# Streamed weight units brought in as two half-partition transfers, and the first four input tiles handled in the plain order

## The chip, the cores and the metric

The kernel runs on one core of a Trainium2 chip. The metric is the device time of one execution in microseconds (us). Before the change three executions took 1972.40, 1976.64 and 1977.27 us; their median is 1976.64.

## What is computed

The reference adds three things: the input x (2048 rows of 1024), a recurrent attention layer over the normalized input, and a dense two-layer network over the same normalized input. Cut to what matters:

```python
xn = layernorm(x)                                  # no scale, no shift
# attention with memory: 64 segments of 32 rows, one after the other
for s in range(64):
    h = concatenate([mem, xn[32*s:32*s+32]])       # 8 memory rows and 32 new rows
    q, k, v = h @ Wq, h @ Wk, h @ Wv               # 1024 -> 32 heads of 128
    p = softmax(masked(q @ k.T * 128**-0.5))
    o = (p @ v) @ Wo                               # 4096 -> 1024
    mem = o[:8]                                    # the next segment needs this
    A[s] = o[8:]
B = gelu(xn @ w1 + b1) @ w2 + b2                   # 1024 -> 3584 -> 1024
out = x + A + B
```

Because a segment's memory rows come out of the segment before, the 64 segments run in order, and each of them passes through all of Wq, Wk, Wv and Wo. In bfloat16 these four are 32 MB, which is more than the on-chip memory holds beside the rest.

## The kernel before

**The dense part** comes first, up to about 420 us. It normalizes x in 16 tiles of 128 rows, transposes each on PE (`turn_x`, L358), and computes the dense network in four groups of four tiles: L481 is the first matrix product, L530 and L563 the second. The results, and the transposed input, are kept in DRAM for the recurrent part.

Before the first product of the first group the first four tiles must be normalized and turned (L436 to L453). Each tile needs statistics on VectorE (`ln_stats`, L323), a square root on ScalarE (`ln_sqrt`, L329), a reciprocal on VectorE (`ln_rstd`, L335), and an application of mean and factor. For tiles 0 to 2 the application is on ScalarE (`ln_apply_scalar`, L346), for tile 3 on VectorE (`ln_apply`, L338). Tiles go one after the other: while one is applied and turned, the statistics of the next are made. PE turns a tile in eight transposes (L362), and two copies (L365), one on VectorE and one on ScalarE, take the result out of PSUM. The scratch tiles for the normalized rows and for the turned rows in PSUM exist twice.

Transfers of this part are nearly all begun by SP, in the order of the program. For the first half of w1, `load_w1` (L292) begins 16 of them: eight for the left half of its columns, then the bias b1 (L302), then eight for the right half. Then come three copies of the masks (L177), four small loads of the memory rows (L308), the bias b2 (L313), the second half of w1, and w2 (L317).

**The recurrent part** is the loop over 64 segments (L658). The four weight matrices are cut into 64 units of 128 partitions by 2048 columns (512 KB, a partition's row 4096 bytes). `pass_order` (L53) lists the units in the order in which each segment uses them. 46 of them stay on the chip for the whole run. The other 18, marked `S` in `PLACED` (L68) and spread over the order, are streamed again for every segment from a contiguous copy of each in DRAM (`copies`, L192, called Wc in the profile). One of the 18 (`IN_PSUM`, L73) is kept in PSUM and is put back by two copies on VectorE (L226) in place of a transfer. Of another (`HALF`, L74) one half stays on the chip, so that its transfer has 256 KB.

Streamed units go through a ring of six tiles (`STREAM_BUFS`, L50). `start_stream` (L220) takes the next tile of the ring and has SP begin the transfer into it (L229):

```python
c0 = 1024 if streams[started] == HALF else 0
nc.sync.dma_start(out=t[:, c0:2048], in_=copies[streams[started]])
```

It is called six times before the loop (L549), and then by `unit_done` (L640) whenever a streamed unit's last product has been issued; so six units are ahead of PE, being transferred or waiting to be used. SP holds a transfer back until PE has finished with the tile, and until the earlier transfer into that tile has landed. Every transfer that SP begins also uses one of eight semaphores, in turn.

PE multiplies a unit with the segment's rows in four products that fill the four quarters of PSUM's partitions (L682 for Wq, Wk, Wv; L861 for Wo). Each contracts over all 128 partitions of the unit. Between them stand the small products of attention (L785 to L841), and the copies that take the results out of PSUM (L725, L848, L940). L940 copies the segment's new memory rows and comes once at the end of every segment but the last.

GpSimd (POOL) begins the recurrent part's small transfers: loads of the next segment's rows (L237, L242), loads of the dense result (L911, L936), and stores. Only at the end do SP and ScalarE store pieces too (L979).

Of the kernel before, what the change touches and what calls it, by code (L numbers as in the profile page):

```python
# [10 lines left out]
BF16 = mybir.dt.bfloat16  # L11
# [67 lines left out]
def kernel(  # L79
# [59 lines left out]
    def slab(place):  # L139
        if place in low:  # L140
            return low[place]
        return slabs.tile([P, 2048], BF16, name="u", tag=place)
# [77 lines left out]
    def start_stream():  # L220
        nonlocal started
        if started < len(streams):
            t = slab(RING[started % STREAM_BUFS])
            if streams[started] == IN_PSUM and "kept" in nxt:
                for b in range(2):
                    nc.vector.tensor_copy(out=t[:, 1024 * b:1024 * b + 1024], in_=nxt["kept"][:, b, :])  # L226
            else:
                c0 = 1024 if streams[started] == HALF else 0
                nc.sync.dma_start(out=t[:, c0:2048], in_=copies[streams[started]])  # L229
            stream_tiles.append(t)  # L230
            started += 1

# [38 lines left out]
    with tc.tile_pool(name="ma", bufs=2) as ma, tc.tile_pool(name="mps", bufs=6, space=PSUM) as mps:  # L271
# [19 lines left out]

        def load_w1(half):  # L292
            for kt in range(KT):
                w1_sb.append(slab(f"w1_{8 * half + kt}")[:, 0:F // 2])
            for c in (0, 1) if half == 0 else (None,):
                for kt in range(KT):
                    cs = slice(0, F // 2) if c is None else slice(F // 4 * c, F // 4 * c + F // 4)
                    nc.sync.dma_start(
                        out=w1_sb[8 * half + kt][:, cs], in_=w1_v[:, kt, F // 2 * half:F // 2 * (half + 1)][:, cs]
                    )  # L300
                if c == 0:
                    nc.sync.dma_start(out=b1rows[:, :], in_=B_b1.rearrange("(fc p) -> fc p", p=P))  # L302

        b1rows = ma.tile([FC, P], BF16, name="b1rows", bufs=1)
        load_w1(0)
        masks_out()
        for j in range(4):
            nc.sync.dma_start(  # L308
                out=o_sb[32 * j + NX:32 * j + 32, 0:8, :],
                in_=mem0[:, 256 * j:256 * j + 256].rearrange("m (h e) -> m h e", h=8),  # L310
            )
        b2row = ma.tile([1, DM], BF16, name="b2row", bufs=1)
        nc.sync.dma_start(out=b2row[:, :], in_=B_b2.rearrange("(o d) -> o d", o=1))  # L313
        load_w1(1)
# [11 lines left out]
                nc.vector.bn_stats(out=stats[:, c, :], in_=xt[:, c * 512:c * 512 + 512])  # L326
            nc.vector.bn_aggr(out=mv[:, tt, :], in_=stats[:, :, :])

        def ln_sqrt(t0, t1):  # L329
            nc.scalar.activation(  # L330
                out=rstd[:, t0:t1], in_=mv[:, t0:t1, 1:2].rearrange("p t o -> p (t o)"), func=ACT.Sqrt,
                bias=eps_t[:, :], scale=1.0,
            )

        def ln_rstd(t0, t1):  # L335
            nc.vector.reciprocal(out=rstd[:, t0:t1], in_=rstd[:, t0:t1])

        def ln_apply(tt):  # L338
            xn = ma.tile([P, DM], BF16, name="ln_xn")
            nc.vector.tensor_scalar(  # L340
                out=xn[:, :], in0=xtoks[tt], scalar1=mv[:, tt, 0:1], scalar2=rstd[:, tt:tt + 1],
                op0=ALU.subtract, op1=ALU.mult,
            )
            return xn

        def ln_apply_scalar(tt):  # L346

            xn = ma.tile([P, DM], BF16, name="ln_xn")
            shift = mv[:, tt, 0:1]
            nc.vector.tensor_scalar(  # L350
                out=shift, in0=shift, scalar1=rstd[:, tt:tt + 1], scalar2=-1.0, op0=ALU.mult, op1=ALU.mult,
            )
            nc.scalar.activation(
                out=xn[:, :], in_=xtoks[tt], func=ACT.Identity, bias=shift, scale=rstd[:, tt:tt + 1],
            )
            return xn

# [76 lines left out]
            ]  # L434

        xnT = new_xnT(0)  # L436
        def begin(tt):
            ln_stats(tt, xtoks[tt])
            ln_sqrt(tt, tt + 1)

        def normed(tt):
            ln_rstd(tt, tt + 1)
            return ln_apply_scalar(tt) if tt < 3 else ln_apply(tt)

        begin(0)
        xns = []
        for tt in range(4):
            if tt < 3:
                begin(tt + 1)
            xns.append(normed(tt))  # L450
            if tt > 0:
                turn_x(tt - 1, xns[tt - 1], xnT)
        turn_x(3, xns[3], xnT)  # L453
        keep_xT(0, xnT)

        b1col = ma.tile([P, FC], F32, name="b1col", bufs=1)
# [6 lines left out]
        for tg in range(4):  # L463
# [46 lines left out]
            if not last:  # L510
                xnT = new_xnT(tg + 1)
                for t in range(4):
                    xtoks[4 * tg + 4 + t] = load_x(4 * tg + 4 + t)
                if tg == 0:
                    for unit, c in copies.items():
                        fetch(c, unit)
                    fetch_resident(*low)
                for t in range(4):
                    ln_stats(4 * tg + 4 + t, xtoks[4 * tg + 4 + t])
                ln_sqrt(4 * tg + 4, 4 * tg + 8)  # L520
                ln_rstd(4 * tg + 4, 4 * tg + 8)
                for t in range(4):
                    ttg = 4 * tg + t
                    xn = ln_apply(ttg + 4)
                    rsb = xtoks[ttg]
                    for nb in range(2):
                        cs = slice(nb * 512, (nb + 1) * 512)
                        ps = mps.tile([P, 512], F32, name="ps")
                        for fc in range(FC):
                            nc.tensor.matmul(  # L530
                                ps[:, :],
                                lhsT=gts[fc // 4][:, fc % 4, t * P:(t + 1) * P],
                                rhs=w2_sb[fc // 2][:, fc % 2, cs],
                                start=(fc == 0),
                                stop=(fc == FC - 1),
                            )
                        nc.vector.tensor_tensor(out=ps[:, :], in0=ps[:, :], in1=b2bc[:, cs], op=ALU.add)
                        nc.vector.tensor_tensor(out=rsb[:, cs], in0=ps[:, :], in1=rsb[:, cs], op=ALU.add)
                        if nb == 1:
                            turn_x(ttg + 4, xn, xnT)  # L540
                    keep_R(ttg, rsb)
                keep_xT(tg + 1, xnT)
                for t in range(4):
                    turn_R(4 * tg + t)
            else:


                for _ in range(STREAM_BUFS):
                    start_stream()  # L549
                fetch_resident(*(place for place in RES_PLACES if place.startswith("w1_")))  # L550
                put_mem(o_sb, nxt["hT"], mps.tile([P, 512], F32, name="ps"))
                pss = [mps.tile([P, 512], F32, name="ps") for _ in range(6)]
                pss += [mps.tile([P, 512], F32, name="pT", bufs=2) for _ in range(2)]
                for n in range(8):
                    cs = slice((n % 2) * 512, (n % 2 + 1) * 512)
                    nc.tensor.matmul(pss[n][:, :], lhsT=ones[0:1, :], rhs=b2row[0:1, cs], start=True, stop=False)
                    nc.tensor.matmul(
                        pss[n][:, :], lhsT=ident, rhs=xtoks[4 * tg + n // 2][:, cs], start=False, stop=False
                    )
                for fc in range(FC):  # L560
                    for t in range(4):
                        for nb in range(2):
                            nc.tensor.matmul(  # L563
                                pss[2 * t + nb][:, :],
                                lhsT=gts[fc // 4][:, fc % 4, t * P:(t + 1) * P],
                                rhs=w2_sb[fc // 2][:, fc % 2, nb * 512:nb * 512 + 512],
                                start=False,
                                stop=(fc == FC - 1),
                            )
                    if fc % 2:  # L570
                        fetch_resident(f"w2_{fc // 2}")
                    if fc % 4 == 3:
                        fetch_resident(f"gT{fc // 4}")
                for n in range(8):
                    cs = slice((n % 2) * 512, (n % 2 + 1) * 512)
                    cp = nc.scalar.copy if n % 2 else nc.vector.tensor_copy
                    cp(out=xtoks[4 * tg + n // 2][:, cs], in_=pss[n][:, :])
                for t in range(4):
                    keep_R(4 * tg + t, xtoks[4 * tg + t])
                fetch_resident("xt2", "xt3")  # L580
# [452 lines left out]
```

## Time and profile before

| what | value |
|---|---|
| median of three executions | 1976.64 us |
| the execution that the profile shows | 1972.4 us, its span 1970.6 us |
| PE busy (matrix products) | 1780.2 us (90%) |
| VectorE (DVE) busy | 854.3 us (43%) |
| ScalarE (ACT) busy | 595.2 us (30%) |
| GpSimd (POOL) busy | 286.5 us (15%) |
| moved by DMA | 644.36 MB, mean 327 GB/s |
| SP's queue | 208,380 packets, 619.26 MB, 83.7% of 16 engines' time |
| chain of waits | PE 65%, DMA 25%, issue 5%, DVE 3%, ACT 1%, POOL 1% |

How to read what follows. The page of the profile shows one execution. Its groups name the line of the kernel, the engine, the operation, and what is written and read (`u` is any tile that holds weights or x, `Wc_K` a unit's copy in DRAM, `acc` a bank of PSUM). The timeline's rows give start and length in us, then engine, line, operation and count; in brackets stands how long the engine was idle before it and what ended that. A window's row gives its length, the busy time of PE, PEld (weight loads of PE), DVE, ACT and POOL with the instructions in brackets, then the granted clock of PE, the busy share of the 16 DMA engines, and GB/s. The view of one line gives shortest, median and longest duration in ns and the first and last start. A row of the waits gives who waited for whom, then the sum in us, how often, and the longest. The trace also holds a record of every DMA packet, with its queue, size, start and length, but not its DMA engine, and the time of every step of a semaphore.

### The profile page before, as it was taken

What the parts mean: (1) busy time and instruction counts of PE and PEld (TensorE: products, weight loads), DVE (VectorE), ACT (ScalarE), POOL (GpSimd) and SP (SyncE); (2) the same over time, 40 slices, a digit from 0 to 9 for tenths busy, and PEclk for the clock granted to TensorE, in tenths of its full rate; (3) what the DMA queues carried; (4) which work ended last, traced back from release to release, by engine and by line L of the source; (5) the groups of instructions that cost most, each with busy time, mean ns of one, the idle gap of its engine ahead of it and who ended that gap; (6) DMA issues with size and microseconds to landing.
All of it is one profiled execution on the core that took longest, in us unless ns stands there. A gap on an engine that the chain in (4) does not pass through costs nothing.

```text
span 1970.6 us, 77144 instructions
## 1 busy us (share of the span) xinstructions
PE 1780.2 (90%) x34271; PEld 974.1 (49%) x34291; DVE 854.3 (43%) x2233; ACT 595.2 (30%) x1352; POOL 286.5 (15%) x557
## 2 busy tenths in 40 slices
PE   7999999999799989888889888888899989888888
PEld 3444444445445544445455545554545455545544
DVE  6656565424344443343434343434344343434433
ACT  6343434312222222232223222222222222222222
POOL 0000000002331111111112111111111111111112
PEclk9999999999999999999999999999999999999999
DMA  9821212789999999999999999999999999999998
GB/s 330 273 55 43 55 43 54 279 305 369 381 355 379 376 384 364 362 384 371 374 378 386 375 396 365 378 380 376 357 391 366 391 371 389 379 380 386 386 374 337
DMA packets 227002, 644.36 MB, mean 327 GB/s; under 512 B 48251, under 2 KB 63915, under 8 KB 226652
## 3 DMA queue, kind: packets, MB, share of 16 engines
q1 hardware_dynamic: 208380, 619.26, 83.7%
q0 software_dynamic: 16928, 18.77, 2.9%
q8 instruction: 268, 4.39, 0.9%
q10 hardware_dynamic: 1360, 1.39, 0.2%
q14 instruction: 66, 0.54, 0.1%
HBM read 625.08 MB, written 31.26 MB: 333 GB/s over the span
## 4 chain that ended last, share of the span: by engine, by line
PE 65%; DMA 25%; issue 5%; DVE 3%; ACT 1%; POOL 1%; POOLq 0%; ACTq 0%; DVEq 0%
PE acc L682 30%; PE acc L861 11%; DMA u<-Wc_O 10%; PE ps L481 10%; DMA u<-Wc_V 7%; PE ps L530 7%; DMA u<-Wc_Q 4%; PE ps L563 2%; DMA u<-Wc_K 1%; PE mixed L835 1%; DMA out_dram<-res 1%; DVE b_oL L739 1%; PE mixed L785 1%; PE acc L835 1%; PE pT L563 1%
## 5 line engine op out<-in xcount | busy, mean ns | idle before, releaser
L682 PE MATMUL acc<-u,hr 128*32 128x512 bf16 x11520 | 795.1, 382 | 37.9 <-DMA u<-Wc_V 13.1
L682 PEld LDWEIGHTS <-hr 128*32 128x32 bf16 x12288 | 356.4, 97 | 315.7 <-issue 75.7
L682 PE MATMUL acc<-u,hrL 128*32 128x512 bf16 x2880 | 261.6, 389 | 6.5 <-issue 4.8
L861 PE MATMUL acc<-u,d_oL 128*32 128x256 bf16 (+1 forms) x3330 | 188.2, 297 | 20.1 <-issue 11.4
L481 PE MATMUL ps<-u 128*128 128x512 bf16 x896 | 196.1, 382 | 2.6 <-ACT u L365 2.6
L861 PE MATMUL acc<-u,b_oL 128*32 128x256 bf16 (+1 forms) x1776 | 129.6, 309 | 46.8 <-DMA u<-Wc_O 28.7
L861 PEld LDWEIGHTS <-b_oL 128*32 128x32 bf16 (+1 forms) x3552 | 118.3, 105 | 105.9 <-issue 71.4
L530 PE MATMUL ps<-u 128*128 128x512 bf16 x657 | 146.2, 379 | 0.8
L481 PEld LDWEIGHTS <-u 128*128 128x128 bf16 x896 | 88.1, 98 | 109.3 <-issue 4.0
L861 PEld LDWEIGHTS <-d_oL 128*32 128x32 bf16 (+1 forms) x3552 | 102.8, 100 | 64.4 <-issue 38.1
L682 PEld LDWEIGHTS <-hrL 128*32 128x32 bf16 x3072 | 93.1, 98 | 64.2 <-issue 24.8
L861 PE MATMUL acc<-W_O,b_oL 128*32 128x256 bf16 (+1 forms) x1776 | 116.2, 311 | 6.5 <-issue 6.5
L911 POOL DMA_DIRECT2D res<-hr_d x64 | 35.8, 559 | 554.8 <-DVE d_oL L848 312.0
L739 DVE STREAM_TRANSPOSE kT<-kT 128x512 bf16<-128x512 bf16 x64 | 45.5, 711 | 161.7 <-ACT kT L725 161.7
L226 DVE COPY u<-kept 128x1024 bf16<-128x1024 bf16 x126 | 81.2, 686 | 72.8 <-PE acc L861 59.7
L835 PEld LDWEIGHTS <-v 32*128 32x128 bf16 x2048 | 63.2, 91 | 96.9 <-issue 73.5
L739 DVE STREAM_TRANSPOSE b_oL<-b_oL 128x512 bf16<-128x512 bf16 x128 | 90.6, 708 | 46.3 <-ACT b_oL L725 46.3
L725 ACT CAST kT<-acc 128x512 bf16<-128x512 f32 x64 | 37.5, 585 | 221.7 <-PE acc L682 221.7
L530 PEld LDWEIGHTS <-u 128*128 128x128 bf16 x672 | 65.3, 98 | 77.3 <-DVE g_u L497 0.4
L848 DVE CAST b_oL<-acc 128x160 bf16<-128x160 f32 x128 | 41.6, 325 | 136.4 <-PE acc L841 136.4
L725 ACT CAST b_oL<-acc 128x512 bf16<-128x512 f32 x128 | 75.4, 589 | 80.3 <-PE acc L682 78.9
L995 POOL DMA_DIRECT2D out_dram<-res x124 | 63.4, 516 | 247.2 <-DVE res L957 246.5
(141 smaller groups left out, 2225.6 us busy)
## 6 DMA issues: line engine op xcount, KB each, us to landing
u<-Wc_O SPq DMA_DIRECT2D x320, 512.0 KB
u<-Wc_K SPq DMA_DIRECT2D x256, 512.0 KB
u<-Wc_V SPq DMA_DIRECT2D x256, 512.0 KB
u<-Wc_Q SPq DMA_DIRECT2D x193, 512.0 KB
u<-Wc_O SPq DMA_DIRECT2D x64, 256.0 KB
u<-in_B_w_dram SPq DMA_DIRECT2D x14, 512.0 KB
u<-in_A_Wq_dram SPq DMA_DIRECT2D x12, 512.0 KB
u<-in_A_Wv_dram SPq DMA_DIRECT2D x12, 512.0 KB
```

What stands on the lines that cost most here:

```text
L226: nc.vector.tensor_copy(out=t[:, 1024 * b:1024 * b + 1024], in_=nxt["kept"][:, b, :])
L481: nc.tensor.matmul(ps[:, :].rearrange("p (s t) -> p s t", t=SEG), lhsT=w1_sb[fb // 14 * 8 + kt][:, (fb % 14) * P:(fb % 14 + 1) * P], rhs=x ...
L530: nc.tensor.matmul(ps[:, :], lhsT=gts[fc // 4][:, fc % 4, t * P:(t + 1) * P], rhs=w2_sb[fc // 2][:, fc % 2, cs], start=(fc == 0), stop=(fc ...
L563: nc.tensor.matmul(pss[2 * t + nb][:, :], lhsT=gts[fc // 4][:, fc % 4, t * P:(t + 1) * P], rhs=w2_sb[fc // 2][:, fc % 2, nb * 512:nb * 512 ...
L682: nc.tensor.matmul(o, lhsT=lhs[:, i, :], rhs=m, start=(i == seq[0]), stop=(i == seq[-1]), tile_position=(0, 32 * j),)
L725: cp(out=out, in_=ps.rearrange("p (h e) -> p h e", e=32))
L739: nc.vector.transpose(out=home, in_=home)
L835: nc.tensor.matmul(oV[b][:, c, :], lhsT=V[q, c * P:(c + 1) * P], rhs=prA[q, c, :], start=(c == 0), stop=False, skip_group_check=True, tile ...
L848: cp(out=outs[u][:, hs, NL * slot:NL * slot + 40], in_=oV[b])
L861: nc.tensor.matmul(acc[r:r + n // 8, 0:n], lhsT=lhs[:, 4 * (i % 4) + 2 * u + k, :], rhs=w_k[:, n * jq:n * jq + n], start=(unit == O_UNITS[ ...
L911: nc.gpsimd.dma_start(out=st["res"][:, :], in_=hr_d[s + 1, :, 256:512])
L995: nc.gpsimd.dma_start(out=out_flat[rows, 256 * j:256 * j + 256], in_=res[32 * j:32 * j + NX, :])
```

## The change

There are two parts. First, the transfer of a streamed unit is begun as two, one for partitions 0 to 63 and one for partitions 64 to 127, each with the same columns as before. Second, the first four input tiles are handled in a plain order: statistics, root and reciprocal for all four tiles; then, for each tile, the application on VectorE and the turn. `ln_sqrt` and `ln_apply_scalar` go, the first half of w1 is loaded in eight transfers of whole rows in place of sixteen, and b1 is loaded after the memory rows. For the later groups of tiles, root and reciprocal are the same two instructions in the same order as before.

```diff
@@ start_stream
                 c0 = 1024 if streams[started] == HALF else 0
-                nc.sync.dma_start(out=t[:, c0:2048], in_=copies[streams[started]])
+                for b in range(2):
+                    ps = slice(64 * b, 64 * b + 64)
+                    nc.sync.dma_start(out=t[ps, c0:2048], in_=copies[streams[started]][ps, :])
@@ load_w1
             for kt in range(KT):
-                w1_sb.append(slab(f"w1_{8 * half + kt}")[:, 0:F // 2])
-            for c in (0, 1) if half == 0 else (None,):
-                for kt in range(KT):
-                    cs = slice(0, F // 2) if c is None else slice(F // 4 * c, F // 4 * c + F // 4)
-                    nc.sync.dma_start(
-                        out=w1_sb[8 * half + kt][:, cs], in_=w1_v[:, kt, F // 2 * half:F // 2 * (half + 1)][:, cs]
-                    )
-                if c == 0:
-                    nc.sync.dma_start(out=b1rows[:, :], in_=B_b1.rearrange("(fc p) -> fc p", p=P))
-
-        b1rows = ma.tile([FC, P], BF16, name="b1rows", bufs=1)
+                t = slab(f"w1_{8 * half + kt}")[:, 0:F // 2]
+                nc.sync.dma_start(out=t, in_=w1_v[:, kt, F // 2 * half:F // 2 * (half + 1)])
+                w1_sb.append(t)
+
         load_w1(0)
         masks_out()
         ...
+        b1rows = ma.tile([FC, P], BF16, name="b1rows", bufs=1)
+        nc.sync.dma_start(out=b1rows[:, :], in_=B_b1.rearrange("(fc p) -> fc p", p=P))
         b2row = ma.tile([1, DM], BF16, name="b2row", bufs=1)
@@ the first four tiles
-        def begin(tt):
+        for tt in range(4):
             ln_stats(tt, xtoks[tt])
-            ln_sqrt(tt, tt + 1)
-
-        def normed(tt):
             ln_rstd(tt, tt + 1)
-            return ln_apply_scalar(tt) if tt < 3 else ln_apply(tt)
-
-        begin(0)
-        xns = []
         for tt in range(4):
-            if tt < 3:
-                begin(tt + 1)
-            xns.append(normed(tt))
-            if tt > 0:
-                turn_x(tt - 1, xns[tt - 1], xnT)
-        turn_x(3, xns[3], xnT)
+            turn_x(tt, ln_apply(tt), xnT)
```

In the new version `ln_rstd` holds both the square root on ScalarE and the reciprocal on VectorE.

More of the change, by code (lines that the diff above doesn't have):

```diff
@@ L327, in ln_stats, with ln_rstd @@
             nc.vector.bn_aggr(out=mv[:, tt, :], in_=stats[:, :, :])
-        def ln_sqrt(t0, t1):
+        def ln_rstd(t0, t1):
+            r = rstd[:, t0:t1]
             nc.scalar.activation(
-                out=rstd[:, t0:t1], in_=mv[:, t0:t1, 1:2].rearrange("p t o -> p (t o)"), func=ACT.Sqrt,
-                bias=eps_t[:, :], scale=1.0,
-            )
-        def ln_rstd(t0, t1):
-            nc.vector.reciprocal(out=rstd[:, t0:t1], in_=rstd[:, t0:t1])
+                out=r, in_=mv[:, t0:t1, 1:2].rearrange("p t o -> p (t o)"), func=ACT.Sqrt, bias=eps_t[:, :], scale=1.0,
+            )
+            nc.vector.reciprocal(out=r, in_=r)
         def ln_apply(tt):
@@ L342, in ln_apply @@
                 op0=ALU.subtract, op1=ALU.mult,
[L343 to L354, printed above, removed]
             )
@@ L519 @@
                     ln_stats(4 * tg + 4 + t, xtoks[4 * tg + 4 + t])
-                ln_sqrt(4 * tg + 4, 4 * tg + 8)
                 ln_rstd(4 * tg + 4, 4 * tg + 8)
```

## The prediction

> **What bounds the kernel now.** I began with the windows of the trace over the recurrent pass, because the page's averages mix it with the dense part:
>
> ```profile
> 490.00:990.00 500.00, 441.92 (x10432) 251.33 (x10428) 198.39 (x527) 139.55 (x354) 102.83 (x191) 0.97 0.99 373
> 990.00:1490.00 500.00, 444.07 (x10655) 256.52 (x10649) 200.98 (x533) 141.67 (x358) 79.58 (x149) 0.99 1.00 379
> 1490.00:1940.00 450.00, 403.01 (x9581) 234.76 (x9584) 181.20 (x483) 127.96 (x324) 74.34 (x140) 0.98 1.00 381
> ```
>
> The last two columns are the busy share of the 16 DMA engines and GB/s. From 490 to 1940 us they are busy 0.99 to 1.00 of the time while PE has 0.88 to 0.90: the pass is bound by DMA. What occupies it stands in the page's list of issues:
>
> ```profile
> u<-Wc_O SPq DMA_DIRECT2D x320, 512.0 KB
> u<-Wc_K SPq DMA_DIRECT2D x256, 512.0 KB
> u<-Wc_V SPq DMA_DIRECT2D x256, 512.0 KB
> u<-Wc_Q SPq DMA_DIRECT2D x193, 512.0 KB
> u<-Wc_O SPq DMA_DIRECT2D x64, 256.0 KB
> ```
>
> That is 1025 whole units and 64 halves, or 16.5 units = 8.65 MB for each of 64 segments, begun by 17 transfers (1089 in all). One segment's length comes from the copy that ends it:
>
> ```profile
> L940 ACT CAST d_oL<-acc x63: 372/372/373, 457.7 to 1942.8; 128x256 bf16<-128x256 f32 x63
> ```
>
> 62 steps in 1485.1 us make 23.95 us. 8.65 MB in that time is 361 GB/s of the 379: the weight stream is 95% of the traffic. The chain of waits agrees (DMA u<-Wc_O 10%, Wc_V 7%, Wc_Q 4%, Wc_K 1%). The trace's packet records say how an engine spends it: between 490 and 1940 us SP's queue has 124,185 packets of 4096 bytes, one partition's row each, median 159 ns, mean 170. A unit is 8 rows and one 4-byte completion packet (9 ns) on each of 16 engines: 16.5 x 8 x 170 ns = 22.4 us, with completions 22.6 of the 23.95; other traffic has 1.35. So any lengthening of these packets lengthens the run one for one.
>
> **The start.** The diff also takes back how the first four input tiles are handled. Now (timeline, first 16 us):
>
> ```profile
> 3.50 1.29 DVE L326 BATCH_NORM_STATS2 ln_stats<-u 128x6 f32<-128x512 bf16 x2 [0.95 <-DMA u<-in_A_x_dram]
> ...
> 13.60 0.55 DVE L340 TENSOR_SCALAR ln_xn<-u,ln_mv,ln_rstd 128x1024 bf16<-128x1024 bf16 x1
> ...
> 14.21 1.03 PE L362 MATMUL pT<-pr_last,ln_xn 128*128 128x128 bf16 x8 [0.55 <-DVE ln_xn L340]
> ...
> 15.91 14.30 PE L481 MATMUL ps<-u 128*128 128x512 bf16 x56 [0.54 <-ACT u L365]
> ```
>
> Dense work begins at 15.9 us, and PE is busy almost throughout after that (73.84 of 74 us in the window 16 to 90), so a delay here is kept. In the new order VectorE does for each tile statistics (1.45 us, first row to next tile's), then waits for ScalarE's root (0.29) and does the reciprocal (0.11), with handovers 2.0 us: four tiles end at 3.5 + 8.0 = 11.5. Then, tile by tile on one in-order VectorE, scaling (0.55), PE's eight transposes (1.03) and a copy (0.42), with handovers 2.05: three rounds, then 0.55 + 1.03 + the last copy on ScalarE 0.58: about 19.9. That is **4 us later**. ScalarE's three applications (1.24 each) go, and cost nothing more. The first matmul now needs whole rows of the first half of w1; x and this half are 4.7 MB, at the 291 GB/s of the window 0 to 16 us landed by about 17, hidden under the 19.9. The bias b1 moves on SP's queue from behind eight weight loads to behind w1, three mask copies and four memory loads, where the other bias starts now at 17.15; landed some 2 us later it is just in time; if not, up to 3 us more. So +4, bounds +2 to +7.
>
> **The split, what is certain.** Each of 1089 transfers becomes two. SP spends 0.32 us on one (L229, median 320 ns): 17 x 2 x 0.32 = 10.9 us of 23.95, with the completion waits between them still room; the second half starts some 0.4 us later, under about 6 us of requests already queued. PE needs both halves before a unit's first product (all 128 partitions are contracted), so nothing starts earlier; a second wait is one more 51 ns semaphore instruction on PE for a unit, 0.9 us a segment, under PE's idle tenth. On each DMA engine one more completion packet: 17 x 9 ns. Matching each packet to the one that ended just before it (the records don't name the engine), the first two packets of a transfer come to 26 ns more than two later ones: at most 17 x 35 ns = 0.6 us a segment, 38 us in all, at least 10.
>
> **The split, what the trace doesn't show.** No sustained load into 64 partitions is in it. How rows are dealt out can be inferred: the four final stores of 24 rows on SP each have 24 packets and 12 completion packets, so 12 engines with two rows each; 64 rows would then go to all 16 engines, four each, and first every engine writes the lower partitions, then every engine the upper. Now each engine has eight partitions to itself. If two engines then share the path that served one, a packet takes up to 2 x 159 = 318 ns; if the path has room, 159. The nearest rows are those 24-row stores (512 bytes a packet): two averaged 37.2 and 34.3 ns, two 27.2 and 27.8, against a median of 27 for this size; single packets reached 58. Crowding thus cost between nothing and 2.1 times. These bursts are 24 packets; the stream is 0.95 of all traffic without a pause, where two engines on one path meet at every packet. I therefore take the far end, less some escape: 3.8% of packets last over 200 ns, on average 265 ns beyond 159, and such a stall puts one engine ahead of its partner. A half of four packets then needs 1272 - 265 = 1007 ns in place of 1272, or 252 ns a packet. A transfer is done when its slowest engine is, so I go nearer the upper value: **294 ns** (1.85 times).
>
> Segment: 16.5 x 8 x 294 = 38.8, completions 17 x 2 x 9 ns = 0.3, other traffic 1.3: 40.4 us, 16.45 more; x 63 (62 steps and the last) = 1036; with the start 1040. On the profiled execution's 1972.4 us (0.2% under the median of 1976.64; span 1970.6) that is 3012, say **3015 us**. PE's 21 to 22 busy us a segment are then far inside.
>
> [...] My 24-row row, taken by its means (27 to 37.2 ns, 1.0 to 1.38 times the 159), would make from no loss up to 16.5 x 8 x 219 = 28.9 us of stream and 2390.
>
> **Rivals.** *Path has room (22%).* For it: two of the four crowded stores lost nothing, and packets that go from memory to memory, without SBUF, also have 159 ns, so that this may be the engine's own pace. Then only completions, first packets and the start are paid: 10 to 38 + 4, about **2000 us** (1980 to 2030).
>
> *Too few requests in flight (12%).* SP's transfers use eight semaphores in turn and wait for the eighth before:
>
> ```profile
> SPq L317 <- DMA u<-in_B_w_dram: 9.1, 12, 1.0
> ...
> SPq L298 <- DMA u<-in_A_x_dram: 1.0, 2, 0.7
> ```
>
> These loads go to fresh tiles and have nothing else to wait for. Today six tiles bound the stream at 3 MB in flight; as halves, eight requests are 2 MB. From issue to the last landing a transfer now takes a median 6.4 us, largely queueing. If that didn't shrink, 2.1 MB per 6.4 us = 328 GB/s, 26.4 us a segment: +2.45 x 63 + 4, about **2130 us**. Against: 2 MB is still 5.5 us of work at 379 GB/s, and 64 to 256 KB transfers in the quiet stretch land in 2.2 us. It decides once unqueued latency is above some 4 us.
>
> *The other side: faster (5%).* The sixteen landings of a transfer are spread over a median 2.2 us, so some engine lags. If its lag lies in the path to its eight partitions, halves give those rows to two engines, and the slow path no longer holds one back. If all packets came to 159 ns: 16.5 x 8 x 11 ns = 1.45 us a segment, -92 + 4: about **1885 us**. It decides only if paths have room for two engines; the even 159 ns median speaks against slow paths.
>
> *No change (6%)*: room in the paths and completions hidden, the start alone: about 1977.
>
> **Numbers.** Shared paths 55%, with their own range from 252 to 318 ns, 2660 to 3220, and milder sharing (1.2 to 1.5 times, 2160 to 2550) in a tenth of that case. Leaving out the two small cases and the ends: 1985 to 3230, wide because the unknown cost has ends a thousand us apart. A run tells about 0.3% from no change: faster 0.05, same 0.07 (the case of no change and the lowest end of the roomy path), slower 0.88.
>
> **What would show it.** Right: in the windows the DMA share stays near 1.00 while GB/s falls to 215 to 270, 4096-byte packets last 250 to 318 ns, PE waits for u at nearly every streamed unit, L940's steps are near 40 us, the first L481 starts near 20 us. Room in the paths: packets near 170 ns, steps under 24.6 us. Too few requests: DMA share below 0.95 with packets unchanged, SP's L229 waiting for DMA more than for PE. I am wrong by the whole of my main term if packets into 64 partitions keep their 170 ns.

## The result and the profile after

The change made the kernel slower: four executions took 2704.34 to 2731.86 us, median 2715.51, against 1975.13 before; the ratio is 1.376, with a 95% interval of 1.368 to 1.383. The forecast was 3015 us, with a range of 1985 to 3230. What follows compares the profiled executions: 2704.3 us with a span of 2702.6 against 1972.4 with 1970.6.

The windows of the recurrent pass after the change, with the same columns as before (length, busy time of PE, PEld, DVE, ACT and POOL, PE's granted clock, DMA share, GB/s):

```profile
490.00:990.00 500.00, 357.33 (x6924) 167.63 (x6928) 132.75 (x352) 91.47 (x235) 78.16 (x145) 0.85 1.03 253
990.00:1490.00 500.00, 365.80 (x7480) 177.58 (x7474) 142.67 (x377) 98.76 (x254) 54.94 (x103) 0.87 1.03 263
1490.00:1990.00 500.00, 357.75 (x7164) 170.71 (x7162) 136.93 (x360) 93.22 (x240) 54.94 (x103) 0.87 1.03 256
```

The 16 DMA engines are as busy as before (1.03: packet records overlap a little now), but move 253 to 263 GB/s in place of 373 to 381. The bytes are the same (644.50 MB against 644.36); so it is the packets that take longer. Between 490 and 2640 us the 4096-byte packets of SP's queue have a median of 261 ns and a mean of 258, where they had 159 and 170. Nine in ten lie between 169 and 315 ns, the upper end about twice the old 159; 4% last over 318 ns (2% before). There are 17,296 more 4-byte completion packets than before. That is 16 for each of the 1089 added transfers, less 16 for each of the eight that w1 lost: 16 for a half, as for a whole unit. This agrees with the prediction's inference that all 16 engines write a half.

The copy that ends a segment, now on L910, and the streamed transfers:

```profile
L910 ACT CAST d_oL<-acc x63: 372/372/373, 476.4 to 2665.2; 128x256 bf16<-128x256 f32 x63
```

```profile
u<-Wc_O SPq DMA_DIRECT2D x640, 256.0 KB
u<-Wc_K SPq DMA_DIRECT2D x512, 256.0 KB
u<-Wc_V SPq DMA_DIRECT2D x512, 256.0 KB
u<-Wc_Q SPq DMA_DIRECT2D x386, 256.0 KB
u<-Wc_O SPq DMA_DIRECT2D x128, 128.0 KB
```

62 steps in 2188.8 us are 35.30 us each, 11.35 more than before. That makes 704 us; the first segment ends 18.7 us later (476.4 against 457.7) and the stretch behind the last step is 9.6 us longer (37.4 against 27.8). The sum is 732 us, the whole difference of the spans.

In the chain of waits the share of DMA rises from 25% to 79%:

```profile
DMA 79%; PE 18%; SPq 1%; DVE 1%; issue 0%; ACT 0%; POOL 0%; POOLq 0%; ACTq 0%
```

The start, in the timeline of the changed kernel: the second tile's statistics begin 1.97 us after the first's, the last scaling begins at 17.90, and the first dense product at 20.20, against 15.91 before.

```profile
3.44 1.28 DVE L323 BATCH_NORM_STATS2 ln_stats<-u 128x6 f32<-128x512 bf16 x2 [0.88 <-DMA u<-in_A_x_dram]
...
5.41 1.27 DVE L323 BATCH_NORM_STATS2 ln_stats<-u 128x6 f32<-128x512 bf16 x2
...
17.90 0.54 DVE L335 TENSOR_SCALAR ln_xn<-u,ln_mv,ln_rstd 128x1024 bf16<-128x1024 bf16 x1
...
20.20 4.00 PE L452 MATMUL ps<-u 128*128 128x512 bf16 x12 [0.54 <-ACT u L348]
```

### The profile page after: what moved, and what is told of

It reads as the page before. It is cut to its first block, busy times and chain, and to the rows that moved or that the text cites. A ratio compares the mean times of both kernels' runs of the same rounds, so it can differ in the third digit from the quotient of the medians.

```text
span 2702.6 us, 78400 instructions
## 1 busy us (share of the span) xinstructions
PE 2039.7 (75%) x34271; PEld 965.2 (36%) x34291; DVE 859.8 (32%) x2233; ACT 585.9 (22%) x1349; POOL 286.9 (11%) x557
## 2 busy tenths in 40 slices
DMA packets 243283, 644.50 MB, mean 238 GB/s; under 512 B 65547, under 2 KB 79163, under 8 KB 242924
## 4 chain that ended last, share of the span: by engine, by line
DMA 79%; PE 18%; SPq 1%; DVE 1%; issue 0%; ACT 0%; POOL 0%; POOLq 0%; ACTq 0%
DMA u<-Wc_O 23%; DMA u<-Wc_Q 20%; DMA u<-Wc_V 20%; DMA u<-Wc_K 14%; PE ps L452 7%; PE ps L500 5%; PE acc L652 3%; DMA hr<-hr_d 1%; PE ps L533 1%; PE acc L831 1%; SPq L231 1%; DMA W_O<-in_A_Wo_dram 1%; DMA u<-in_A_Wo_dram 0%; PE pT L345 0%; DMA u<-in_A_Wv_dram 0%
## 5 line engine op out<-in xcount | busy, mean ns | idle before, releaser
L652 PE MATMUL acc<-u,hr 128*32 128x512 bf16 x11520 | 881.6, 401 | 358.8 <-DMA u<-Wc_V 163.1
L652 PEld LDWEIGHTS <-hr 128*32 128x32 bf16 x12288 | 322.4, 101 | 792.4 <-DMA u<-Wc_V 179.1
L831 PE MATMUL acc<-u,b_oL 128*32 128x256 bf16 (+1 forms) x1776 | 147.0, 371 | 217.2 <-DMA u<-Wc_O 215.5
L652 PE MATMUL acc<-u,hrL 128*32 128x512 bf16 x2880 | 298.8, 466 | 0.0
L831 PE MATMUL acc<-u,d_oL 128*32 128x256 bf16 (+1 forms) x3330 | 226.4, 341 | 54.3 <-DMA u<-Wc_O 52.4
L831 PEld LDWEIGHTS <-d_oL 128*32 128x32 bf16 (+1 forms) x3552 | 110.6, 113 | 129.9 <-DMA u<-Wc_O 57.6
L831 PE MATMUL acc<-W_O,b_oL 128*32 128x256 bf16 (+1 forms) x1776 | 135.6, 370 | 1.1 <-issue 1.1
L910 ACT CAST d_oL<-acc 128x256 bf16<-128x256 f32 x63 | 23.4, 372 | 477.5 <-PE acc L831 477.5
L452 PEld LDWEIGHTS <-u 128*128 128x128 bf16 x896 | 87.9, 98 | 108.7 <-issue 4.0
L652 PEld LDWEIGHTS <-hrL 128*32 128x32 bf16 x3072 | 90.1, 111 | 68.4 <-issue 36.6
L790 ACT ACTIVATE mixed<-mixed 128x160 f32<-128x160 f32 x128 | 36.9, 288 | 308.3 <-PE mixed L786 308.3
```

The lines of the kernel that those rows point to most:

```text
L452: nc.tensor.matmul(ps[:, :].rearrange("p (s t) -> p s t", t=SEG), lhsT=w1_sb[fb // 14 * 8 + kt][:, (fb % 14) * P:(fb % 14 + 1) * P], rhs=x ...
L652: nc.tensor.matmul(o, lhsT=lhs[:, i, :], rhs=m, start=(i == seq[0]), stop=(i == seq[-1]), tile_position=(0, 32 * j),)
L790: nc.scalar.activation(out=dA, in_=dA, func=ACT.Ln)
L831: nc.tensor.matmul(acc[r:r + n // 8, 0:n], lhsT=lhs[:, 4 * (i % 4) + 2 * u + k, :], rhs=w_k[:, n * jq:n * jq + n], start=(unit == O_UNITS[ ...
```

## Experiments

The theory to test: the loss comes from which partitions are written at the same time, because all 16 DMA engines crowd into the paths to one half of the partitions. A path is here the way into a group of partitions; it is inferred, no row of the trace names it. The rivals: twice as many transfers cost too much in themselves, or leave too few bytes in flight; or a transfer of 64 rows is slow as such, whatever its rows are. Each experiment changes L229 of the kernel before, except where its diff says otherwise. Packet figures are for 4096-byte packets of the streaming queue between 490 and 1700 us.

### The two parts alone

Only the split, with the old start:

```diff
-                nc.sync.dma_start(out=t[:, c0:2048], in_=copies[streams[started]])
+                for b in range(2):
+                    ps = slice(64 * b, 64 * b + 64)
+                    nc.sync.dma_start(out=t[ps, c0:2048], in_=copies[streams[started]][ps, :])
```

> The split alone, with the start as before. Both theories (two engines share a path; twice as many transfers cost too much) put the whole loss into the split: 2704.3 less the 4.3 us by which the first dense product came later (20.20 against 15.91 us) is 2700 for a profiled execution and 2711 for the median. If the plain start costs more than its 4 us later on, this run falls below 2700.

Measured: 2720.49 us, ratio 1.381 (1.376 to 1.385). The whole loss is here. The 4 us that the old start should have saved don't show; the executions of the split spread over 20 us (2716.7 to 2736.4), too much to see them.

Only the start, with whole units (the change without the edit above):

> The plain start alone, units whole. Expected: 4.3 us slower than before, 1979 against 1975 (ratio 1.002), the first dense product at 20.2 us. If the recurrent pass absorbs the delay (it is bound by DMA, and the first streamed units are fetched before the dense part ends): no difference.

Measured: 1978.24 us against 1973.61, ratio 1.003 (1.001 to 1.005): 4.6 us, with an interval of about 2 to 10. This agrees with the 4.3 us of the later first product; a sign that something later takes it back is not seen.

### As many transfers, but of 128 partitions

```diff
-                nc.sync.dma_start(out=t[:, c0:2048], in_=copies[streams[started]])
+                cm = (c0 + 2048) // 2
+                for c in (slice(c0, cm), slice(cm, 2048)):
+                    nc.sync.dma_start(out=t[:, c], in_=copies[streams[started]][:, c.start - c0:c.stop - c0])
```

> Each unit begun as two transfers again, but cut by columns: both have 128 partitions with rows of 2048 bytes. Number of transfers, semaphores and bytes in flight are those of the change. Theory of shared paths: packets of 2048 bytes stay near 86 ns (what HALF's packets take before), so 16.5 x 16 x 86.3 ns = 22.8 us of stream in a segment, with completions and other traffic 24.4 to 24.7 us: 2000 to 2025. Theory of too many transfers or too few bytes in flight: about 2700, as the change.

Measured: 2045.48 us, ratio 1.037 (1.034 to 1.039). A window and the steps of this kernel:

```profile
990.00:1490.00 500.00, 442.73 (x10142) 238.50 (x10138) 191.86 (x510) 134.76 (x341) 77.50 (x145) 0.98 1.01 361
```

```profile
L942 ACT CAST d_oL<-acc x63: 372/372/374, 461.4 to 2017.1; 128x256 bf16<-128x256 f32 x63
```

With the change's number of transfers, semaphores and bytes in flight, the engines move 361 GB/s and a segment takes 25.09 us, 1.14 more than before. By the sum the shorter packets account for all of this: 16.5 x 16 x 90.1 ns = 23.8 us against 22.4. So doubling the count costs at most 1.14 of the change's 11.35 us, even with this extra price. It came out 20 us above the expected range, because 2048-byte packets averaged 90.1 ns and not 86.3. So the number of transfers and the bytes in flight are ruled out as the cause of the large loss.

### The same 64 rows into two places

Both kernels bring half a unit, with the same 64 source rows; one into partitions 0 to 63, one into 32 to 95. The first six transfers are whole, and the six ring tiles are kept under one name each. The first kernel (the second has 32 and 96 for 0 and 64):

```diff
+                ps, src = slice(0, 64), slice(0, 64)
+                if started < STREAM_BUFS:
+                    ps = src = slice(0, P)
-                nc.sync.dma_start(out=t[:, c0:2048], in_=copies[streams[started]])
+                nc.sync.dma_start(out=t[ps, c0:2048], in_=copies[streams[started]][src, :])
```

> Half of each unit is left out: after the first six, a streamed transfer brings 64 rows of the copy into partitions 0 to 63 alone, and the rest of the tile keeps old data. 17 transfers of 256 KB in a segment. Shared paths: the 16 engines meet in the paths of the lower side all the time, so packets come near the full price where the queue holds work, 270 to 318 ns; 16.5 x 4 x 300 = 20 us of stream a segment, hidden under PE's 21 to 22: 1800 to 1900 us. Otherwise packets stay at 159 to 175 ns.

> As the run into partitions 0 to 63, with the same 64 source rows, the same number and size of transfers, but into partitions 32 to 95. Half of each unit is left out again. If paths belong to the sides of the memory (below and above partition 64) and neighbouring rows go to one engine, each engine has a path to itself: packets 159 to 175 ns, 1790 to 1860 us. If 64 rows as such, or the source in DRAM, make packets long, they are as long here as into 0 to 63.

Measured: 1901.44 us for partitions 0 to 63, 1750.55 for 32 to 95 (one execution each; the kernel before had a median of 1975.8 beside them). One window of each, first 0 to 63:

```profile
990.00:1490.00 500.00, 459.45 (x11057) 267.21 (x11052) 211.36 (x560) 147.85 (x374) 82.53 (x155) 0.99 0.95 205
```

then 32 to 95:

```profile
990.00:1490.00 500.00, 492.47 (x12412) 290.20 (x12403) 233.33 (x624) 164.76 (x417) 93.55 (x176) 1.00 0.75 230
```

With half of the stream left out, writing to 0 to 63 still keeps the engines 0.95 busy at 205 GB/s: packets have a median of 314 ns, 1.97 times 159. The same rows in 32 to 95 need 0.75 of the engines for more bytes a second, and the median is 159 ns, as with whole units. Source, row length, number and size of the transfers are equal; only the partitions written differ. This is the experiment that settles the cause: which partitions are written makes the packets long. It also fits the inferred dealing out, in which neighbouring rows go to one engine, four to each, and the paths below partition 64 are apart from those above it; the records name neither an engine nor a path, so this stays an inference. The second kernel has PE 0.98 busy and is then bound by PE; it came out 40 us below the expected range, the first 1 us above its own.

One thing stays open: into 32 to 95 a tenth of the packets still last over 379 ns, so that the mean is 209. The engines often run out of work there; whether such a packet includes waiting for a request was not tried.

### How long the engines stay on one side

The split alone, with every second unit's halves in the other order, so that by the inferred dealing out an engine writes eight packets in a row on a side (lower, upper, upper, lower, lower, ...):

```diff
-                for b in range(2):
+                for b in (0, 1) if started % 2 else (1, 0):
```

> The split with the order of the halves swapped for every second unit: lower, upper, upper, lower, lower, upper. Each side is then written for eight packets of an engine in a row in place of four. If engines are mostly in step and gain only what one stall puts them ahead (my prediction's picture), a stall frees a smaller share of a longer stretch: packets rise from 258 to some 285 ns, 2900 us. If the engines stand at random against each other, the length of a stretch changes nothing: 2700, within 1%.

Measured: 2902.55 us, ratio 1.470 (1.463 to 1.478), as expected for engines that are mostly in step; packets 279 ns on average (285 expected), median 288. With engines at random against each other, 2700 was expected.

Then four transfers of 32 partitions for a unit, with the sides in turn (two packets on a side) or in order (0, 32, 64, 96: four on a side, as in the change):

```diff
-                nc.sync.dma_start(out=t[:, c0:2048], in_=copies[streams[started]])
+                for p0 in (0, 64, 32, 96):
+                    ps = slice(p0, p0 + 32)
+                    nc.sync.dma_start(out=t[ps, c0:2048], in_=copies[streams[started]][ps, :])
```

> Four transfers of 32 partitions for a unit, the sides in turn: 0 to 31, 64 to 95, 32 to 63, 96 to 127. An engine writes two packets on one side, then two on the other. Series so far: four packets on a side 258 to 260 ns, eight 279, all on one side 296. If the length of the stretch on a side sets how often engines meet, two packets give about 245 ns: 16.5 x 8 x 245 = 32.3 us of stream and some 35 a segment with completions, about 2600 to 2680, and 80 to 150 us less than the quarters in order. If the number of transfers or the megabyte left in flight (eight quarters are two units) decides, both run alike, at 2800 or more.

> The same four transfers in the order 0 to 31, 32 to 63, 64 to 95, 96 to 127, so that an engine has four packets on a side in a row, as in the change; all else as with the sides in turn. Stretch theory: packets near 260 ns as in the change, 2720 to 2850 with the price of two more transfers for a unit. If the number of transfers decides, the same time as with the sides in turn.

Measured: 2792.05 us in turn (1.414, 1.407 to 1.422), 2941.16 in order (1.491, 1.483 to 1.498). A window of each, in turn first:

```profile
990.00:1490.00 500.00, 354.89 (x6996) 177.84 (x6996) 131.93 (x347) 90.45 (x231) 52.40 (x98) 0.84 0.88 247
```

```profile
990.00:1490.00 500.00, 346.65 (x6516) 169.44 (x6512) 126.14 (x333) 85.81 (x221) 52.60 (x99) 0.82 0.97 234
```

The order alone is worth 149 us, at the upper end of what the sides in turn were expected to save (80 to 150). Packets average 227 ns in turn and 261 in order. Both times lie above the expected ranges, and the DMA share says why: 0.88 and 0.97 against 1.03 in the change. The engines run dry here. Eight requests of a quarter unit are only 1 MB, but with the sides in turn that is not what SP waits for. Its waits for landings between 990 and 1490 us are short:

```profile
SPq L231 <- DMA u<-Wc_O: 9.9, 40, 0.9
SPq L231 <- DMA u<-Wc_K: 3.8, 16, 0.5
SPq L231 <- DMA u<-Wc_Q: 3.6, 14, 0.7
SPq L231 <- DMA u<-Wc_V: 2.3, 13, 0.3
```

They make 20 of 500 us, while SP spends 420 us on beginning 934 transfers (median 0.419 us each). So here SP can hardly begin transfers fast enough. In order it is 363 us for 882 transfers and 83 us of waits for landings. Whether 1 MB in flight would be too little by itself is not shown. Mean packet by packets in a row on one side:

| packets in a row on a side (inferred) | kernel | mean ns |
|---|---|---|
| 2 | quarters in turn | 227 |
| 4 | the split alone; quarters in order | 260; 261 |
| 8 | order swapped | 279 |
| all | partitions 0 to 63 alone | 296 |

The first row is not quite comparable: with the engines idle for 12% of the time, they may also meet less often.

### Half of the unit into partitions 32 to 95

```diff
-                nc.sync.dma_start(out=t[:, c0:2048], in_=copies[streams[started]])
+                for ps in (slice(32, 96), slice(0, 32), slice(96, 128)):
+                    nc.sync.dma_start(out=t[ps, c0:2048], in_=copies[streams[started]][ps, :])
```

> The whole unit again, as three transfers: partitions 32 to 95, 0 to 31, 96 to 127. Shared paths: half of the bytes (32 to 95) at about 175 ns a packet, half crowded at about 258: mean 216, 16.5 x 8 x 216 = 28.5 us of stream, about 30.3 a segment, 2375 us; faster than the change although it has three transfers. Number of transfers or bytes in flight (eight transfers are now 2.7 units): slower than the change, 2800 or more.

Measured: 2722.21 us, ratio 1.379 (1.375 to 1.384). This misses the 2375 that the theory gave, and also the 2800 or more of the rival. Packets average 246 ns, not 216; a quarter are under 191, so that by the theory some run alone, but most don't.

```profile
990.00:1490.00 500.00, 362.34 (x7148) 181.23 (x7140) 135.73 (x357) 92.68 (x238) 53.15 (x100) 0.85 0.99 251
```

The expectation treated crowding as a property of a transfer. If crowding is a matter of the moment, a packet into 32 to 95 is alone only while no other engine is at that path with rows of the ends; engines several transfers apart would often break this. How far apart they are was not measured here (in the changed kernel the 16 landings of a half are spread over a median 3.7 us). That reading fits the quarter of short packets, but is argued; no run isolates it.

### The upper half on another queue

```diff
-                nc.sync.dma_start(out=t[:, c0:2048], in_=copies[streams[started]])
+                for b, eng in enumerate((nc.sync, nc.scalar)):
+                    ps = slice(64 * b, 64 * b + 64)
+                    eng.dma_start(out=t[ps, c0:2048], in_=copies[streams[started]][ps, :])
```

> The split as in the change, but the upper half is begun by ScalarE on its own queue, so that each DMA engine has two queues with work and can take them in turn, and 16 transfers can be in flight. Shared paths with engines at random: packets for both sides are mixed, two engines meet in a path about half of the time as now, 240 to 260 ns, 2600 to 2720. If they settle into opposite turns, packets near 170 to 200 and 2000 to 2250. If eight requests in flight were the limit: near 2000 with packets unchanged in the change. ScalarE's waits for a tile may delay its own work by some us a segment.

Measured: 2743.87 us, ratio 1.390 (1.386 to 1.394). Packets average 265 ns on SP's queue and 267 on ScalarE's, above the 240 to 260 expected for engines at random, and far above the 170 to 200 for opposite turns; twice the requests in flight gain nothing. ScalarE now waits for transfers itself, so that the time above the split alone (2720.49) can have this cause too:

```profile
ACT d_oL L942 <- DMA u<-Wc_Q: 296.4, 44, 9.7
...
ACT mixed L822 <- DMA u<-Wc_V: 229.1, 56, 6.6
...
ACT d_oL L727 <- DMA u<-Wc_V: 150.7, 49, 4.4
```

No version that did the whole work came below the kernel before.

## Why the prediction was right, point by point

**The number and the signs.** The range of 1985 to 3230 held the rivals as well, so that the time fell into it says little; the main case's own range, 2660 to 3220, holds it near its lower end. The signs say more. GB/s (253 to 263, forecast 215 to 270), the DMA share (1.03), the mean packet (258 ns, forecast 250 to 318) and the first dense product (20.20 us) are as forecast; the steps are 35.30 us and not "near 40".

**What bounds the pass.** Right: the step was worked out from the packets' time, and putting the measured 258 ns into that sum gives 16.5 x 8 x 258 ns + 1.6 us = 35.7 us, which is 11.7 more than before; 1972.4 + 11.7 x 63 + 4 = 2714, where 2704 was measured. Nothing else in the pass was needed to explain it.

**The start.** Right: +4 was forecast from the rows, 4.3 stands in the timeline, 4.6 (2 to 10) in the runs of the start alone. The bias b1 was in time (SP begins it at 16.36, PE turns it at 19.46).

**The certain part of the split.** The cost of completions and first packets was hidden in the larger term; the columns bound it, with shorter packets included, at 1.14 us a segment. SP's price for a transfer was wrong: 0.445 us, not 0.32, for 64 rows. This is not seen to have cost anything, because SP still waits 997 us in all for landings:

```profile
SPq L231 <- DMA u<-Wc_O: 329.4, 542, 2.2
SPq L231 <- DMA u<-Wc_V: 254.5, 468, 1.9
SPq L231 <- DMA u<-Wc_K: 238.3, 413, 2.2
SPq L231 <- DMA u<-Wc_Q: 175.1, 332, 2.0
```

These rows alone look like my rival of too few requests, one of whose signs they were to be. The other two signs, a DMA share below 0.95 and unchanged packets, are absent: here SP waited that long at a share of 1.03.

**The shared paths.** Right in that the partitions written set the packet's length, shown by the pair of runs into 0 to 63 and 32 to 95 (median 314 and 159 ns); that engines share a path there is the inference that fits it. The mis-sized term is the packet: 294 ns were forecast, 258 measured, 38.8 us of stream against 34.1. The step that failed is "a transfer is done when its slowest engine is, so I go nearer the upper value". The engines don't wait for one another at each transfer: the 16 landings of one are spread over a median 3.7 us (2.2 before), where a whole unit takes 2.1. So a stall that puts an engine ahead may be kept for many packets; this is a reading, no run isolates it. The lower of my two values, 252 ns for a lead of one stall, would have given about 2665. That it lies so near is partly luck: it takes one stall of 265 ns off every half, while only 3.8% of packets had one. The same sum gives 285 ns for eight packets on a side (279 measured), but about 185 for two, where 227 were measured although the engines were idle for 12% of the time. The series supports that engines on one side are mostly in step; it doesn't confirm the sum.

**Rivals.** The roomy path is refuted by packets of 314 ns. Too few requests in flight is refuted for the change by the columns (2 MB in flight, share 1.01); at 1 MB the engines run dry, but there SP's own time for beginning transfers stands in the way of a verdict. Nothing was faster.

**The rate of the stream.** The run into 0 to 63 moved 4.33 MB of stream in steps of 22.73 us (the copies that end its segments go from 461.4 to 1870.7), 190 GB/s (205 with the other traffic). The changed kernel's stream moves 8.65 MB in 35.30 us, 245 GB/s, where it had 361 before.

## What to carry to other kernels

Where DMA engines are busy all the time, judge a change of a transfer's shape by how long a packet takes, not by the engines' share: here it was 1.03 with packets of 258 ns on average, and 0.99 to 1.00 before with 170. Transfers of 64 rows to partitions 0 to 63 and 64 to 127 took 1.38 times the whole kernel's time here (the split alone, 2720.49 us against 1973.61). If only 64 rows are needed, partitions 32 to 95 were the better place (one run of each here: median packet 159 ns, mean 209, against 314 and 296 into 0 to 63); if 128 are, one transfer for all of them is the form to keep: the seven others tried here took 1.037 to 1.491 times its time.

## What was not expected of the hardware

PE's granted clock fell from 0.98 of full speed to 0.879 over the run, while PE's busy share fell from 90% to 75%. This row of the changed kernel's page shows it, in tenths per slice:

```profile
PEclk9999999877898898988888978888888898988878
```

The trace's clock records hold only the values 1.0 and 0.5. There are 90 stretches at 0.5, and all but the last have a length of 3.41 us or a multiple of it, up to 20.48. Products on L652 have the median of before, 379 ns, but 14% of them last over 600 (1.5% on L682 before). No run separates what this cost; with a DMA share of 1.03 little is to be expected. What starts a stretch is not shown: between 480 and 2600 us PE never paused for more than 2.74 us between products, and in the 3.41 us before each of the 83 stretches that begin and end there it was busy for 0.18 to 0.63 of the time.

SP's time for a transfer differed with the partitions written: the medians are 0.32 us for 128 (the kernel before), 0.445 for 64 from partition 0 or 64 (the changed kernel), and 0.489 for 64 from partition 32 (the run into 32 to 95).
